# A planned attention-and-gating kernel: own planning keys for early loads, clearing and fillers, and a new table of keys

## The chip, the cores and the metric

The kernel runs on one core of a Trainium2 chip. The metric is the device time of one execution in microseconds, the median of several runs; less is better. The engines are TensorE (PE in the profile; its weight loads are PEld), VectorE (DVE), ScalarE (ACT), GpSimd (POOL) and SyncE (SP), whose queue starts every transfer of this kernel.

## The reference

Sparse attention (8 batches of 8 heads, 576 positions, 64 wide) feeds a gated feed-forward layer that also mixes over positions:

```python
scores = scale * q @ k.T                    # per head
attn   = softmax(where(mask, scores, -1e9)) # 4 heads: the last 32 positions; 4 heads: every 32nd position
x      = (attn @ v) as [8, 576, 512]
h      = relu(x @ w_in)                     # [8, 576, 1024]
u, v   = halves of h
v_n    = (v - mean(v)) / sqrt(var(v) + 1e-6)
v_s    = w_spatial @ v_n + b_spatial        # mixes the 576 positions of a batch
out    = (u * v_s) @ w_out                  # [8, 576, 512]
```

## The kernel before, in words

Two heads are worked together, so a batch has four "head pairs", and head pair t = 4*batch + hp. Pairs 0 and 1 of a batch are local (scores by 36 small products, L507; attn @ v by L617), pairs 2 and 3 are strided (L650 and L720). The softmax of a pair is a chain over DVE and ACT: a reduce for the maximum, exponentials on ACT (L564, L687), a sum, a reciprocal and a product (L469), then a transpose on DVE into the buffer `pc` (L588 local, L704 strided). There is one `pc` buffer, one `ptl` and one `pts`: ACT and POOL copy the transposed blocks into them (L412 on ACT and L414 on POOL are the two forms of one copy), and attn @ v reads them. Its result is moved out of PSUM in two float32r parts, the rounded value (L434, ACT) and what is left (L422, DVE).

Every matrix is kept as such a pair of parts, and a product is three matmuls (`PROD`). Helper `rnd` makes the first part (L412/L414), `rest` the second (L422). The weights arrive as 64-bit words: `words` turns them into float32 by an ACT instruction (L789), a POOL instruction (L798) and a DVE instruction (L806), and `parts` splits them. For w_in there are eight such pieces, for w_out four, from which seven combined blocks are made (`weight_blocks`, L825). `spatial_weights` loads the four row blocks of w_spatial into `wsp_sb`, numbered 0 to 3 here, and the last 64 rows with the bias into `wt_h` and `wt_b` (L905).

A batch has then three stages on PE. Stage 1 (`moe_1`): 4 tiles of v (L957, 128x512), normalised by `chain` (L915, L920 to L940) into `vn`, then 8 tiles of u (L999, 128x288). Stage 0 (`moe_tail`): the last 64 positions. Stage 2 (`moe_2`): `spatial` (L1079, with L1091 and L1092 for the last 64 positions), whose results multiply u on DVE (L1101), then the product with w_out (L1168) in seven partial products, and the stores.

Nothing of the order is written out by hand. Each step is handed to `Program.add` with a key, the engines that could do it with a cost for each, and what it reads and writes. `Program.order` then steps through time with these costs: when an engine is free it takes the ready step with the lowest key, and a step that several engines could do goes where it would end first. `SLOWED` says by how much DVE and POOL steps that run together slow each other. `Program.fillers` looks at the finished plan: where PE would be idle for over `WARM_GAP` before a marked step, it puts products of zeros (L1349, `warm`) ahead of that step, `WARM_SHARE` of the gap long at `WARM_COST` each. What comes out is one fixed order for each engine; on the chip each engine follows its own order and waits where an input is late. The table `KEYS` holds the keys of the first eight head pairs (`a`), of the weight pieces and their loads, of the clearing of buffers (`fill`) and of the steps inside stage 2 (`p`, `b`).

Every load goes through the one SP queue in planned order (`load`, L442), so a load whose buffer is not yet free holds up those behind it.

Of the kernel before, what the change touches and what calls it, by code (L numbers as in the profile page):

```python
# [37 lines left out]
TAIL = S - 4 * P  # L38
NT = 4
KEYS = {  # L40
    "a": (-7906.0, -7964.0, -15830.5, -4267.6, 1379.5, 702.2, 2039.1, -3334.8,),
    "v": (5971.0, -3908.5, -3534.4, 726.2,),
    "u": (4329.4, -8322.8, -3410.6, -6121.6,),
    "s": (13308.3, 1709.1, 5210.5, 13961.2,),
    "t": (2702.5,),
    "o": (1519.5, 3986.0, -8051.8, 12581.5,),
    "cst": (-11921.6,),
    "lead": (-1.3,),
    "fill": (-7688.6, 5328.4, -10489.4, 9430.7, 11172.9, 3859.6,),
    "dp": (12894.8, -1038.4,),  # L50
    "dpt": (657.16,),
    "lv": (-2858.0, -4582.1, -8989.4, -1041.3,),
    "lu": (66.6, -1740.1, -5229.0, 1297.1,),
    "lo": (-7685.9, 12601.4, 4211.2, 6006.6,),
    "ls": (3541.9, 11770.0, 12130.5, 1637.8, 8461.5,),
    "near": (4868.39,),
    "p": (2.79, 10.51, 0.21,),
    "b": (25.62, -1.03, 29.44, -12.2, 10.78, 11.69, 33.63, 25.64, -64.18, 15.47, 14.89,),
}
WARM_END, WARM_GAP, WARM_COST, WARM_COLS, WARM_SHARE = 110000.0, 700.0, 427.0, 256, 0.8  # L60
PE_MASKED, APART = (0, 1, 2, 3), (0, 1)
OTHER_BANK = (1, 2, 3)
FETCHED, FETCH_COST = 100.0, 32.0
SLOWED = ((0.3, 0.15), (0.45, 0.6), (0.9, 0.8))
DMA_RATE, DMA_ISSUE, DMA_LAG, DMA_TAIL, TABLE_LOAD = 370.0, 470.0, 1500.0, 500.0, 1280.0
PROD = ((0, 0), (0, 1), (1, 0))
BLOCKS = ("a11", "a12", "a22", "s1", "s2", "s3", "s4")
# [82 lines left out]
class Program:  # L150
# [39 lines left out]
    def order(self):  # L190
# [14 lines left out]
        held_by = {DVE: (0.0, 0.0, 0, None), POOL: (0.0, 0.0, 0, None)}  # L205
        peer = {DVE: POOL, POOL: DVE}

        def shared(n, e, at, cost):

            if e in self.port.get(n, ()):  # L210
                since, until, share, _ = held_by[peer[e]]
                if since <= at < until:
                    both = min(until - at, cost)
                    slow = SLOWED[max(share, self.share[n])]
                    return (slow[0] * both, slow[1] * both) if e == DVE else (slow[1] * both, slow[0] * both)
            return 0.0, 0.0

# [14 lines left out]
        while len(issued) < len(ops):  # L232
# [57 lines left out]
            if e in self.port.get(n, ()):  # L290
                more, theirs = shared(n, e, now, cost)
                cost += more
                p = peer[e]
                begun, until, share, m = held_by[p]
                if theirs and free[p] == until:
                    free[p] = until = until + theirs
                    held_by[p] = (begun, until, share, m)
                    for j in after[m]:
                        for o in ENGINES:
                            ready_at[j][o] = max(ready_at[j][o], until + LAT[p][o])  # L300
                held_by[e] = (now, now + cost, self.share[n], n)
            free[e] = end = now + cost
            if e == DMA:
                moved = max(moved, now + DMA_LAG) + self.bytes[n] / DMA_RATE
# [13 lines left out]
    def fillers(self, issued):  # L318


        ends, free, found = {}, 0.0, {}
        for at, n, e in issued:
            cost = dict(self.ops[n][1])[e]
            ends[n] = at + cost
            if e == PE:
                if n in self.spare and at < WARM_END:
                    before = self.spare[n][0].before
                    gap = at - max([free, 600.0, *(ends[m] + 200.0 for m in before)])
                    if gap > WARM_GAP:
                        found[n] = int(WARM_SHARE * gap / WARM_COST)  # L330
                free = at + cost
        return found

# [14 lines left out]
def attention_moe(ctx, tc, qT, kT, ks, vl, vs, cst, eye, w_in, w_out, wsp, wtail, out):  # L348
# [91 lines left out]
    def load(key, dst, src, writes, nbytes, reads=()):  # L440
        add(
            key, [(DMA, DMA_ISSUE)], lambda eng: eng.dma_start(dst(), src), reads, writes,  # L442
            size=nbytes,
        )
# [297 lines left out]
    def attention(t, due):  # L742
# [7 lines left out]
            v = lambda: f32(place()).rearrange("p a b c -> p (a b c)").rearrange("p (u d) -> p u d", d=D)  # L750
        else:
            v = place = r_v.new()
        load(due - 34, q, qT[b, hp], [(q,)], P * SP * 4)
        if local:
            k = r_k.new()
            load(due - 33, k, kT[b, hp], [(k,)], P * (STRIDE + S) * 4)
            load(due - 20, lambda: v()[:, : 2 * LB, :], vl[b, hp], [(place,)], P * 768 * 4)
            kin = [(k,)]
        else:
            for j in range(2):  # L760
                load(
                    due - 33, lambda j=j: kbd[j::2, t % 2, j, STRIDE:],
                    ks[b, hp - 2, j], [("k", t % 2, j)], 64 * S * 4, [("k0", t % 2)],
                )
            load(due - 20, v, vs[b, hp - 2], [(place,)], P * 1024 * 4)
            kin = [("k", t % 2, j) for j in range(2)]
        xs[t] = r_x.new()
        (local_attention if local else strided_attention)(t, due, q, k, v, [(place,)], kin)
# [49 lines left out]
    def weight(key, fetch, src, n, dst, tok, stage):  # L818
        val, _, reads = words(key, fetch, src, n, stage)
        parts(key, n, val, dst, reads, tok)  # L820
# [488 lines left out]
    for h in range(2):  # L1309
# [2 lines left out]
            [("k0", h)],  # L1312
        )
        add(
            -90, [(DVE, 250), (POOL, 400)],
            lambda eng, h=h: (
                eng.memset(p_local[h]()[64:, 2 * LS - 2 :, :], 0.0),
                eng.memset(st_local[h]()[64:, NU + 2 * LS - 2 : NU + 2 * LS], 0.0),
# [4 lines left out]
    fill(KEYS["fill"][0], ptl, 2 * LB * LQ, ("ptl0",))  # L1323
    fill(KEYS["fill"][1], pts, NU * 4 * RA, ("pts0",))
    add(-250, [(DVE, 100)], setup_sel, (), [("sel",)])
    add(-100, [(POOL, 1200)], setup_ones, (), [("ones",)])

    def due(t):
        if t < len(KEYS["a"]):
# [104 lines left out]
```

## Time and profile before

| | before |
|---|---|
| time, median of 3 runs | 519.44 us (519.14 to 519.69) |
| the profiled execution | 519.78 us, of which its span is 517.7 us |
| PE busy | 499.6 us of the span |
| DVE, ACT, POOL busy | 363.0, 267.4, 129.0 us |
| moved by transfers | 52.65 MB |

The profile shows one execution. The span runs from the first to the last instruction; the 2.1 us by which the execution's time is longer lie outside it. Rows of the timeline start with the start time and the duration in us, then the engine, the line of the source, what is written and read, the count of merged instructions, and in brackets the idle time of the engine before it and what ended it. A float32r or float32 matmul of the program is one row in the order; a float32 one is two matmuls in the trace.

### The profile page before, as it was taken

The numbers are of one execution on the slowest core, as the hardware profiler recorded it, in microseconds if no ns is written. First come the engines' busy times: TensorE is split into PE (matmuls) and PEld (weight loads), VectorE is DVE, ScalarE is ACT, GpSimd is POOL, SyncE is SP. The second block draws the span as 40 slices with busy tenths as digits, with TensorE's granted clock in tenths as the row PEclk, the third lists the DMA queues.
The fourth block names the chain that finished last, engine by engine and source line by source line (L and its number), as shares of the span: only waits on it lengthen the run. The fifth ranks groups of instructions, "written<-read, shape, count | busy, mean of one in ns | idle before, by whom it ended". The sixth has DMA issues, their size and how long they took to land.

```text
span 517.7 us, 14663 instructions
## 1 busy us (share of the span) xinstructions
PE 499.6 (97%) x5884; PEld 459.3 (89%) x5884; DVE 363.0 (70%) x1093; ACT 267.4 (52%) x825; POOL 129.0 (25%) x245
## 2 busy tenths in 40 slices
PE   6779889999999999999999999999999999999997
PEld 3558779979999899998999899998999889998997
DVE  2899989969479747896369764897457861676156
ACT  5786765568554476456336276366446252233222
POOL 3355864043212121312102111233102120102000
PEclk9689979999999999999999999999999999999999
DMA  8897323454024322262023422063011300020002
GB/s 274 307 343 268 125 83 90 149 164 151 2 79 151 118 79 81 85 180 84 11 69 121 148 80 80 1 209 113 1 56 53 123 1 1 1 80 13 1 1 91
DMA packets 26243, 52.65 MB, mean 102 GB/s; under 512 B 3136, under 2 KB 11584, under 8 KB 26176
## 3 DMA queue, kind: packets, MB, share of 16 engines
q1 hardware_dynamic: 26176, 51.72, 30.3%
q8 instruction: 46, 0.75, 0.6%
q14 instruction: 21, 0.17, 0.1%
HBM read 42.27 MB, written 9.44 MB: 100 GB/s over the span
## 4 chain that ended last, share of the span: by engine, by line
PE 89%; DVE 4%; DMA 2%; ACT 2%; SPq 1%; POOL 1%; issue 1%; POOLq 0%
PE m L1079 20%; PE m L957 18%; PE m L1168 18%; PE m L999 18%; PE po L720 4%; PE po L617 3%; PE s L507 3%; PE s L650 2%; PE m L1091 2%; PE m L1092 2%; DMA k<-kT 1%; SPq L442 1%; DMA x<-wsp 1%; PE po L1349 1%; DVE w_in_sb L422 0%
## 5 line engine op out<-in xcount | busy, mean ns | idle before, releaser
L1079 PE MATMUL m<-wsp_sb,vn 128*128 128x288 f32 x768 | 113.3, 300 | 4.3 <-DVE wsp_sb L422 4.3
L1079 PEld LDWEIGHTS m<-wsp_sb,vn 128*128 128x128 f32 x768 | 107.3, 192 | 5.4 <-DVE wsp_sb L422 4.6
L999 PE MATMUL m<-x,w_in_sb 128*128 128x288 f32 x768 | 105.3, 297 | 0.0
L999 PEld LDWEIGHTS m<-x,w_in_sb 128*128 128x128 f32 x768 | 103.4, 188 | 1.2
L957 PE MATMUL m<-w_in_sb,x 128*128 128x512 f32 (+1 forms) x408 | 99.5, 399 | 0.0
L957 PEld LDWEIGHTS m<-w_in_sb,x 128*128 128x128 f32 (+1 forms) x408 | 74.5, 186 | 19.0 <-DVE x L422 0.2
L1168 PE MATMUL m<-g,w_out_sb 128*128 128x288 f32 x384 | 56.9, 298 | 0.0
L414 POOL TENSOR_SCALAR ptl<-pc 32x64 f32<-32x64 f32 (+3 forms) x89 | 37.9, 426 | 64.7 <-DVE pc L588 24.2
L1168 PEld LDWEIGHTS m<-g,w_out_sb 128*128 128x128 f32 x384 | 52.3, 188 | 1.0 <-ACT vv L434 0.3
L422 DVE TENSOR_TENSOR x<-po,x 128x288 fp32r<-128x288 f32 x64 | 27.6, 447 | 36.3 <-ACT x L434 35.6
L1101 DVE TENSOR_TENSOR u<-m,u 128x288 f32<-128x288 f32 x64 | 28.1, 453 | 30.9 <-PE m L1092 30.7
L564 ACT ACTIVATE pl<-pl,ml 128x64 f32<-128x64 f32 (+1 forms) x140 | 47.0, 339 | 4.7 <-DVE ml L544 4.3
L915 ACT ACTIVATE vv<-m 128x512 f32<-128x512 f32 (+1 forms) x37 | 22.0, 596 | 45.7 <-PE m L957 39.6
L412 ACT CAST g<-u 128x288 fp32r<-128x288 f32 x46 | 19.2, 434 | 50.2 <-DVE u L1101 49.0
L933 POOL TENSOR_TENSOR bn<-bn,sel 128x1 f32<-128x1 f32 (+1 forms) x37 | 21.1, 575 | 95.0 <-DVE bn L928 77.0
L1013 ACT ACTIVATE u<-m 128x288 f32<-128x288 f32 x64 | 25.7, 408 | 35.0 <-PE m L999 34.6
L1168 PE MATMUL m<-vn,w_out_sb 128*128 128x288 f32 x288 | 42.6, 297 | 0.0
L920 DVE BATCH_NORM_STATS2 bn<-vv 128x6 f32<-128x512 f32 (+1 forms) x37 | 25.3, 683 | 21.0 <-ACT vv L915 20.5
L1168 PEld LDWEIGHTS m<-vn,w_out_sb 128*128 128x128 f32 x288 | 39.5, 188 | 0.4
L434 ACT CAST x<-po 128x288 fp32r<-128x288 f32 x64 | 24.7, 397 | 26.2 <-PE po L617 14.4
L412 ACT COPY ptl<-pc 32x64 f32<-32x64 f32 (+3 forms) x103 | 35.7, 346 | 4.7 <-DVE pc L588 2.6
L422 DVE TENSOR_TENSOR g<-u,g 128x288 fp32r<-128x288 f32 x64 | 27.0, 449 | 7.9 <-ACT g L412 6.2
(131 smaller groups left out, 726.6 us busy)
## 6 DMA issues: line engine op xcount, KB each, us to landing
q<-qT SPq DMA_DIRECT2D x30, 295.0 KB, 4.2
outT<-o SPq DMA_DIRECT2D x48, 144.0 KB, 2.7
v_raw<-vs SPq DMA_DIRECT2D x13, 512.0 KB, 4.2
v_raw<-vl SPq DMA_DIRECT2D x16, 384.0 KB, 3.7
k<-kT SPq DMA_DIRECT2D x16, 304.0 KB, 4.5
kbd<-ks SPq DMA_DIRECT2D x32, 144.0 KB, 4.6
outT<-vv SPq DMA_DIRECT2D x16, 144.0 KB, 3.7
vn<-w_in SPq DMA_DIRECT2D x4, 512.0 KB, 4.5
```

Of the source, the lines that this page charges most:

```text
L412: eng.copy(dst(), src())
L414: eng.tensor_scalar(dst(), src(), 1.0, 0.0, op0=ALU.mult, op1=ALU.add)
L422: eng.tensor_tensor(dst(), src(), f32(hi()), op=ALU.subtract)
L434: eng.copy(dst(), src())
L564: eng.activation(p_sb()[:m, u, :], src, AF.Exp, bias=st()[:m, u : u + 1], scale=SCALE if masked else -1.0, **total,)
L920: lambda eng: eng.bn_stats(bn()[:m, 0:6], v()[:m]), [(v,)], [(bn,)],
L957: eng.matmul(v_ps()[:m, :], x_at(kt)[:, a, :], w_in_sb[:, w, kt, HF:], start=(n == 0 and i == 0), stop=(n == NT - 1 and i == 2),)
L999: eng.matmul(u_ps()[:, :HS], w_in_sb[:, w, kt, f * P : (f + 1) * P], xs[NHP * b + kt]()[:, a, r], start=(n == 0 and i == 0), stop=(n == NT ...
L1013: lambda eng, u=u, f=f, u_ps=u_ps: eng.activation(u()[:, f * HS : (f + 1) * HS], u_ps()[:, :HS], AF.Relu),
L1079: eng.matmul(s_ps()[:, :HS], vn()[:, a, kt, fs], wsp_sb[:, w, kt, r], start=(kt == 0 and i == 0), stop=False,)
L1101: lambda eng, ug=ug, s_ps=s_ps: eng.tensor_tensor(ug(), s_ps()[:, :HS], ug(), op=ALU.mult),
L1168: eng.matmul(o_ps()[:, :HS], w_out_sb()[:, b_at, w, kk, a * P : (a + 1) * P], at(j, kk), start=first and kk == 0 and i == 0, stop=kk == 1 ...
```

## The change

`attention` takes the keys of the first loads of the first eight head pairs (q and k from `lq`, v from `lw`) out of the table; before, they were the pair's own key less 34, 33 and 20. The clearing of the local buffers and the setting of the ones in `tails_b` take their keys from `set` (before, -90 and -100), with other POOL costs. `fillers` takes its end, least gap and share from `w`. In the account of the port that DVE and POOL share, a step on POOL that is not a plain copy now counts with weight 2, and the three factors of `SLOWED` are others. All other numbers of `KEYS` are new as well.

```diff
-    "a": (-7906.0, -7964.0, -15830.5, -4267.6, 1379.5, 702.2, 2039.1, -3334.8,),
+    "a": (-9842.3, -13561.9, -6739.1, -5352.0, 1588.0, 1874.9, 6528.0, -115.1,),
...
+    "lq": (-15760.0, -16334.1, -13342.4, -5854.6, 690.8, 3109.9, 6338.5, -4265.1,),
...
+    "set": (3904.8, 1535.2, 5000.2,),
+    "w": (73.2, 1.25, 0.82,),
 }
-WARM_END, WARM_GAP, WARM_COST, WARM_COLS, WARM_SHARE = 110000.0, 700.0, 427.0, 256, 0.8
+WARM_COST, WARM_COLS = 427.0, 256
...
-SLOWED = ((0.3, 0.15), (0.45, 0.6), (0.9, 0.8))
+SLOWED = ((0.45, 0.2), (0.6, 0.5), (0.95, 0.5))
...
+        def weight(n, e):
+            return 2 if e == POOL and self.share[n] else self.share[n]
+
...
-                    slow = SLOWED[max(share, self.share[n])]
+                    slow = SLOWED[max(share, weight(n, e))]
...
-                held_by[e] = (now, now + cost, self.share[n], n)
+                held_by[e] = (now, now + cost, weight(n, e), n)
...
+        until, least, share = KEYS["w"]
...
-                if n in self.spare and at < WARM_END:
+                if n in self.spare and at < until * 1000.0:
...
-                    if gap > WARM_GAP:
-                        found[n] = int(WARM_SHARE * gap / WARM_COST)
+                    if gap > least * 1000.0:
+                        found[n] = int(share * gap / WARM_COST)
...
-        load(due - 34, q, qT[b, hp], [(q,)], P * SP * 4)
+        early = t < len(KEYS["lq"])
+        first = KEYS["lq"][t] if early else due - 34
+        last = KEYS["lw"][t] if early else due - 20
+        load(first, q, qT[b, hp], [(q,)], P * SP * 4)
...
-            -90, [(DVE, 250), (POOL, 400)],
+            KEYS["set"][1 + h], [(DVE, 250), (POOL, 260)],
...
-    add(-100, [(POOL, 1200)], setup_ones, (), [("ones",)])
+    add(KEYS["set"][0], [(POOL, 1060)], setup_ones, (), [("ones",)])
```

The order of the program shows what these numbers do. Line numbers are higher by 8 to 11 after the change, by which L442 becomes L450, L507 L515, L650 L658, L617 L625, L720 L728, L957 L968, L1079 L1090 and L1349 L1360.

The SP queue at the start of the program, before; `w_out_sb` and `xt` lend their room to early q and v, and `vn_101` is where the first piece of w_in lands:

```order
L442 DMA w_out_sb_84<-qT 128x590
L442 DMA xt_87<-vs 128x1024
L442 DMA cst_sb<-cst 128x192
L442 DMA o_97<-eye 128x128
L442 DMA vn_101<-w_in 128x1024
L442 DMA kbd<-ks 64x576 x2
L442 DMA q_123<-qT 128x590
L442 DMA k_134<-kT 128x608
L442 DMA v_raw_140<-vl 128x768
L442 DMA q_176<-qT 128x590
L442 DMA k_181<-kT 128x608
```

The same place after the change; `g_88` is where the first piece of w_in lands:

```order
L450 DMA cst_sb<-cst 128x192
L450 DMA o_85<-eye 128x128
L450 DMA g_88<-w_in 128x1024
L450 DMA q_95<-qT 128x590
L450 DMA k_101<-kT 128x608
L450 DMA q_109<-qT 128x590
L450 DMA k_130<-kT 128x608
L450 DMA xt_138<-vs 128x1024
L450 DMA w_out_sb_178<-qT 128x590
L450 DMA kbd<-ks 64x576 x2
```

The first k of a local pair moves from the ninth transfer to the fifth and the second from the twelfth to the seventh; q, v and the two `kbd` halves of a strided pair, which led, now follow them.

PE early in the program, before, from the end of the second local scores on:

```order
L507 MATMUL s_131<-k_181,q_176 32x64
L1349 MATMUL po_292<-zeros 32x256 x3
L720 MATMUL po_292<-pts,xt_87 64x4x18 x8
L720 MATMUL po_304<-pts,xt_87 64x4x18 x8
L650 MATMUL m_136<-kbd,w_out_sb_84 32x36 x32
L957 MATMUL m_385<-w_in_sb,x_331 128x512 x3
```

The same place after the change:

```order
L515 MATMUL s_127<-k_130,q_109 32x64
L658 MATMUL m_133<-kbd,w_out_sb_178 32x36 x32
L1360 MATMUL po_319<-zeros 32x256 x9
L625 MATMUL po_319<-ptl,v_raw_225 64x96 x6
L625 MATMUL po_339<-ptl,v_raw_225 64x96 x6
L658 MATMUL m_135<-kbd,w_out_sb_178 32x36 x32
L1360 MATMUL po_415<-zeros 32x256 x4
L625 MATMUL po_415<-ptl,v_raw_237 64x96 x6
```

The two local pairs now come first and a strided pair third, where a strided pair was first; thirteen fillers stand between them instead of three (at the very start six instead of eight), and the first tile of v comes after both local pairs.

PE at the start of `spatial` of the first batch, before, from the last product of the tile of the last 64 positions on:

```order
L957 MATMUL m_992<-w_in_sb,x_584 64x512 x3
L1079 MATMUL m_1021<-wsp_sb,vn_768 128x288 x12
L1079 MATMUL m_1042<-wsp_sb,vn_768 128x288 x12
L1079 MATMUL m_1065<-wsp_sb,vn_768 128x288 x12
L1079 MATMUL m_1084<-wsp_sb,vn_768 128x288 x12
```

The same place after the change:

```order
L1090 MATMUL m_1026<-wsp_sb,vn_816 128x288 x3
L1090 MATMUL m_1032<-wsp_sb,vn_816 128x288 x3
L1090 MATMUL m_1038<-wsp_sb,vn_816 128x288 x3
L1090 MATMUL m_1026<-wsp_sb,vn_816 128x288 x9
L1090 MATMUL m_1032<-wsp_sb,vn_816 128x288 x9
L1090 MATMUL m_1038<-wsp_sb,vn_816 128x288 x9
L1090 MATMUL m_1091<-wsp_sb,vn_816 128x288 x12
```

The three products of row block 0 of w_spatial are taken first for three of the tiles, nine in all, and row blocks 1 to 3 follow; before, each tile took its twelve products in one go.

More of the change, by code (lines that the diff above doesn't have):

```diff
@@ L40 @@
 KEYS = {
-    "a": (-7906.0, -7964.0, -15830.5, -4267.6, 1379.5, 702.2, 2039.1, -3334.8,),
[L42 to L58, printed above, removed]
+    "a": (-9842.3, -13561.9, -6739.1, -5352.0, 1588.0, 1874.9, 6528.0, -115.1,),
+    "v": (3324.6, -3241.3, 9582.3, -5209.5,),
+    "u": (1292.4, -8773.3, 1053.3, -7394.3,),
+    "s": (2510.3, 5363.0, 3093.9, 7327.8,),
+    "t": (3012.2,),
+    "o": (3704.2, 5299.5, -4144.6, 3282.7,),
+    "cst": (-27014.0,),
+    "lead": (-1.28,),
+    "fill": (831.9, 1735.9, -6584.2, 7746.1, -10956.1, -3358.7,),
+    "dp": (10150.7, -1069.6,),
+    "dpt": (1659.05,),
+    "lv": (-3549.0, -10121.4, -23802.2, 253.8,),
+    "lu": (-1364.4, 547.0, -7064.7, 2152.9,),
+    "lo": (1371.6, 1303.1, 10963.2, -2623.4,),
+    "ls": (11951.3, 14222.0, 7837.0, 4330.3, 14728.9,),
+    "near": (7082.92,),
[4 rows of a table added]
+    "set": (3904.8, 1535.2, 5000.2,),
+    "w": (73.2, 1.25, 0.82,),
 }
-WARM_END, WARM_GAP, WARM_COST, WARM_COLS, WARM_SHARE = 110000.0, 700.0, 427.0, 256, 0.8
+WARM_COST, WARM_COLS = 427.0, 256
 PE_MASKED, APART = (0, 1, 2, 3), (0, 1)
@@ L752, in attention @@
             v = place = r_v.new()
-        load(due - 34, q, qT[b, hp], [(q,)], P * SP * 4)
+        early = t < len(KEYS["lq"])
+        first = KEYS["lq"][t] if early else due - 34
+        last = KEYS["lw"][t] if early else due - 20
+        load(first, q, qT[b, hp], [(q,)], P * SP * 4)
         if local:
             k = r_k.new()
-            load(due - 33, k, kT[b, hp], [(k,)], P * (STRIDE + S) * 4)
-            load(due - 20, lambda: v()[:, : 2 * LB, :], vl[b, hp], [(place,)], P * 768 * 4)
+            load(first + 1, k, kT[b, hp], [(k,)], P * (STRIDE + S) * 4)
+            load(last, lambda: v()[:, : 2 * LB, :], vl[b, hp], [(place,)], P * 768 * 4)
             kin = [(k,)]
@@ L761, in attention @@
                 load(
-                    due - 33, lambda j=j: kbd[j::2, t % 2, j, STRIDE:],
+                    first + 1, lambda j=j: kbd[j::2, t % 2, j, STRIDE:],
                     ks[b, hp - 2, j], [("k", t % 2, j)], 64 * S * 4, [("k0", t % 2)],
                 )
-            load(due - 20, v, vs[b, hp - 2], [(place,)], P * 1024 * 4)
+            load(last, v, vs[b, hp - 2], [(place,)], P * 1024 * 4)
             kin = [("k", t % 2, j) for j in range(2)]
```

3 rows, old and new, of the table KEYS are left out of this document.

## Prediction

> **What bounds the kernel now.** I read the busy shares first, then PE's share and clock over the span.
>
> ```profile
> PE 499.6 (97%) x5884; PEld 459.3 (89%) x5884; DVE 363.0 (70%) x1093; ACT 267.4 (52%) x825; POOL 129.0 (25%) x245
> PE   6779889999999999999999999999999999999997
> PEclk9689979999999999999999999999999999999999
> ```
>
> PE is busy nearly everywhere; what it lacks lies in the first six of the 40 slices, where the clock is reduced too. The busy times of four stretches (PE, PEld, DVE, ACT, POOL, then clock and transfers) say who is short there.
>
> ```profile
> 0.00:25.00 25.00, 18.03 (x352) 11.54 (x354) 12.29 (x32) 15.71 (x42) 9.22 (x24) 0.80 0.82 288
> 25.00:67.00 42.00, 34.63 (x467) 29.07 (x462) 41.27 (x111) 32.44 (x92) 27.88 (x38) 0.94 0.71 246
> 67.00:86.00 19.00, 18.79 (x197) 18.46 (x198) 17.50 (x40) 10.43 (x36) 10.27 (x15) 0.87 0.27 83
> 86.00:518.00 432.00, 428.16 (x4876) 400.19 (x4874) 291.91 (x914) 208.85 (x658) 81.64 (x169) 1.00 0.24 78
> ```
>
> From 86 us on PE misses 3.84 us, which is the end of the program (last results out and stored). From 25 to 67 us DVE is busy 41.27 of 42 us: it sets the pace of the ramp, and PE waits. PE's own waits show where they meet.
>
> ```profile
> PE m L1079 <- DVE wsp_sb L422: 4.3, 1, 4.3
> ```
>
> PE's timeline around that one wait, and DVE's:
>
> ```profile
> 59.87 2.94 PE L957 MATMUL m<-w_in_sb,x 128*64 128x512 f32 x12
> 62.64 0.29 PE L1079 MATMUL m<-wsp_sb,vn 128*128 128x288 f32 x1
> 67.21 8.65 PE L1079 MATMUL m<-wsp_sb,vn 128*128 128x288 f32 x47 [4.28 <-DVE wsp_sb L422]
> ```
> ```profile
> 65.75 2.08 DVE L422 TENSOR_TENSOR wsp_sb<-x,wsp_sb 128x576 fp32r<-128x576 f32 x3
> ```
>
> I call 67.21 the gate: PE has done stage 1 of the first batch and sits until DVE has made the low part of row block 0 of w_spatial, the second of the three rests that start at 65.75. From the gate on PE never waits for long. So the time is the gate, plus the PE work behind it.
>
> **Behind the gate nothing changes but eight matmuls.** The PE order after the change holds the same work on both sides of the gate; only that nine products of row block 0 now stand ahead of the wait (one was there before), and 39 instead of 47 follow. In later batches, at full clock, 48 matmuls of 512 columns and 96 of 288 columns (the size of these nine) take this long, in the chain of work that ended last:
>
> ```profile
> 231.84 11.20 PE m L957 x48
> 243.04 12.79 PE m L999 x96
> ```
>
> 12.79/96 = 0.133 us (and 11.20/48 = 0.233 for the wide ones), so the gate's far side is 8 x 0.133 = 1.07 us shorter. The later stages take slightly different orders with the new `p` and `b`, around which PE had no idle time (428.16 of 432 us with the end counted); DVE has 292 of 432 us of work there, so I count them at nothing. If that cover were gone, each wait for a late part would cost its own length, and seven changeovers from stage 2 to stage 1 would show it.
>
> **The gate is DVE's work plus its idle and lengthened time.** Up to the gate DVE has 142 instructions in both orders, of the same kinds, except that one rest of w_spatial has gone to POOL and the rest for `wt_b` has come ahead of the gate, both 0.74 us long. Before, the gate is the 141st of them, after it is the 142nd: 0.67 us (start to start) is lost there. So the question is how much sooner the start gets DVE going, and whether it is disturbed more.
>
> Before, DVE's start is this:
>
> ```profile
> 7.85 0.69 DVE L806 SCALAR_TENSOR_TENSOR vn<-vn 128x512 int32<-128x512 int32 x1 [6.96 <-POOL vn L798]
> 12.56 0.49 DVE L527 TENSOR_REDUCE ml<-m 128x5 f32<-128x320 f32 x1 [1.54 <-PE m L507]
> 27.52 0.78 DVE L422 TENSOR_TENSOR x<-po,x 128x288 fp32r<-128x288 f32 x2
> ```
>
> Adding the unhindered start-to-start times of each kind (0.60 us for 128x512, 0.37 for 288 columns, 0.76 for a local transpose and so on), the work ahead of the row at 27.52 is worth 13.3 us, and that up to the second rest 43.8. What is done by 27.52 before equals what the new order has done with its 33rd DVE row, the transpose of the first strided pair. When is that reached? These rows carry it, first the k's transfer (KB each, us to landing):
>
> ```profile
> k<-kT SPq DMA_DIRECT2D x16, 304.0 KB, 4.5
> ```
> ```profile
> 2.57 0.43 SPq L442 DMA_DIRECT2D vn<-w_in  x1
> 6.17 0.43 SPq L442 DMA_DIRECT2D k<-kT  x1
> 7.59 0.43 SPq L442 DMA_DIRECT2D k<-kT  x1
> 11.20 1.34 PE L507 MATMUL m<-k,q 64*32 64x64 f32 x72 [1.65 <-DMA k<-kT]
> 13.82 1.12 PE L507 MATMUL s<-k,q 64*32 64x64 f32 x59 [1.27 <-DMA k<-kT]
> 14.06 2.10 ACT L564 ACTIVATE pl<-m,ml 128x64 f32<-128x64 f32 x10 [2.50 <-DVE ml L535]
> 25.29 0.81 DVE L469 TENSOR_TENSOR pl<-pl,ml 128x640 f32<-128x640 f32 x1
> 27.62 2.54 ACT L412 COPY ptl<-pc 32x320 f32<-32x320 f32 x7
> 24.67 1.28 PE L617 MATMUL po<-ptl,v_raw 128*64 128x96 f32 x24 [0.32 <-POOL g L798]
> ```
>
> The first k was issued at 6.17 and its scores began at 11.20, 5.03 us on; the second k took 6.2 us (7.59 to 13.82). The fifth transfer of a queue that doesn't wait is issued where the w_in piece stood, at 2.57, the seventh 0.94 later, at 3.51. So the local scores begin at about 7.6 and 9.7 instead of 11.2 and 13.8. The maxima follow 1.36 us behind (9.0 and 11.1, with 0.9 us of DVE each), the exponentials at 10.2 to 12.3 and 12.3 to 14.4 (2.10 per set), sum, reciprocal and product (0.73, 0.13, 0.81 start to start) by 14.3, the second sum by 15.3, the first transpose by 16.0. Its thirteen block copies, split between ACT and POOL, take 2.5 us, so the second transpose can start at 18.7, since there is one `pc`. The first attn @ v starts at 18.9 and ends at 20.2; the second copies follow, behind ACT's two casts of the first result, until 23.7, and the 33rd DVE row runs from 23.8 to 24.45. That is 3.07 us ahead of 27.52. The clearing of `pts` goes from ACT to POOL, ahead of the first word step there:
>
> ```profile
> 2.11 2.17 POOL L1290 MEMSET kbd<- 128x1216 f32 x2
> 7.14 0.64 POOL L798 TENSOR_SCALAR vn<-vn 128x512 int32<-128x512 uint8 x1 [2.85 <-DMA vn<-w_in]
> ```
>
> POOL was done clearing at 4.28 and waited 2.85 us for the piece; about 1.1 us more ends at 5.4, ahead of the piece, which now lands near 6.2, so it costs nothing. Of the queue's late half, the loads that wait for PE (the k of the third local pair, the v of the fourth) land six or more us ahead of their use.
>
> From there the rest of the way is 43.8 - 13.3 = 30.5 us of DVE work before; it took from 27.52 to the gate's rest, which ends 0.3 us ahead of 67.21, so 39.4 us, 1.29 for each. What lengthens it is POOL:
>
> ```profile
> 42.02 1.75 POOL L422 TENSOR_TENSOR wsp_sb<-x,wsp_sb 128x576 fp32r<-128x576 f32 x1
> 42.39 1.92 DVE L422 TENSOR_TENSOR w_in_sb<-vn,w_in_sb 128x512 fp32r<-128x512 f32 x1
> 15.62 0.92 POOL L414 TENSOR_SCALAR pts<-pc 32x288 f32<-32x288 f32 x2 [7.84 <-DVE pc L704]
> 54.06 1.00 POOL L414 TENSOR_SCALAR wt_h<-x 128x576 fp32r<-128x576 f32 x1
> ```
>
> The DVE rest of 0.60 us took 1.92, to just after POOL's rest had ended. Up to the gate POOL has one rest of w_spatial more after the change (1.75), a copy for w_in more and one for vn less, no `wt_h` (-1.00), and two `pts` copies less (0.46 each): together about nothing. I keep 1.29. The Trainium skill (SBUF — State Buffer, "SBUF: two separate sides") says that of a DVE step with two SBUF inputs and a POOL step that reads SBUF, whichever starts first holds a port pair for its whole length and the other is fully blocked. The row at 42.39 agrees: 0.60 us of work ended 0.55 us behind POOL's. By this rule the added POOL rest speaks against the change and costs up to 1.75 us more: a gate at 66.8 and a time of 518.0.
>
> So the gate comes at 24.45 + (30.5 + 0.67) x 1.29 + 0.3 = 65.0 us, 2.2 sooner. PE itself gets there at about 61.8: the last v tile needs the w_in and x rests at DVE's 51st and 54th rows (10.6 us of work on, 24.45 + 10.6 x 1.29 = 38.1), then 15 v matmuls at 0.233, 96 of u at 0.133, a strided attn @ v and local scores 2.05, its wait for `pts` 1.3, the tail tile 2.8 and nine products 1.2. It then idles 3.2 us instead of 4.28, so I leave the slow clock behind the gate as it is.
>
> **The sum.** 519.78 (profiled execution) - 2.2 (gate) - 1.07 (eight matmuls) = 516.5. The median of before lies 0.34 below its profiled run, so **516.2 us**. The loads may land 0.5 us sooner (4.5 us is the k's median) or 1 us later, and the factor may lie between 1.18 and 1.35, the latter with the whole POOL rest added (41.15/30.5). Sooner and 1.18 give a gate at 61.0, but PE is not there before 61.6; later and 1.35 give 67.8. That makes 512.8 to 519.0 for this case.
>
> **Rivals.** (A, chance 0.57) The sum above, faster. (B, 0.13) The lengthening shrinks, since the new plan charges more for the overlaps, to 1.18 or less: the gate then falls to 24.45 + 31.2 x 1.18 + 0.3 = 61.6, where PE arrives, its wait and the slow matmuls behind it go (47 in 8.65 us instead of 6.26, so 2.4 us): about 511 to 513 (519.78 - 5.6 - 1.07 - 0.34 = 512.8, and 510.4 with all of the slow clock gone). For it speaks the many DVE rows of 0.9 us and more for 0.5 us of work; against it, that POOL has as much to do. (C, 0.13) The lead of 3 us is lost again by the gate, because the later loads, behind PE's releases, come no sooner: only -1.07 + 0.67, so 519.4 and, on the median, 519.0, no change. Against it: from 25 us on DVE was idle for 0.73 of 42 us only, so it was not waiting for loads there.
>
> (D, 0.17) Slower: the fillers run at half clock and overrun the gap they fill. Nine calls, 18 matmuls, stand ahead of the first attn @ v, and four more ahead of the second.
>
> ```profile
> 3.50 0.18 PEld L1349 LDWEIGHTS m<-zeros 128*32 128x32 f32 x1 [0.25 <-issue]
> 3.88 1.62 PEld L1349 LDWEIGHTS m<-zeros 128*32 128x32 f32 x8 [0.21 <-issue]
> ```
> ```profile
> 16.39 0.46 PE L507 MATMUL s<-k,q 64*32 64x64 f32 x13 [1.45 <-issue]
> 16.78 2.77 PE L1349 MATMUL po<-zeros 128*32 128x256 f32 x6
> 19.48 1.88 PE L720 MATMUL po<-pts,xt 128*64 128x72 f32 x32
> ```
>
> Before, six of them took 2.77 us, 0.46 each, and the product behind them began at 19.48, though POOL's copies for it ended at 16.54: about two us were lost there already. With the strided scores done at 12.5 and a stall like the 1.45 us at 16.39, 18 at 0.46 last from 14.0 to 22.3, 3.4 us past the 18.9 above, and eight more cost another us: DVE's 33rd row then ends at 28.85, the gate comes at 69.4, and the time is 519.78 + 2.2 - 1.07 - 0.34 = 520.6. Against it: at the very start the first fillers came 0.43 apart and, from 3.88 on, eight in 1.62 us (0.20 each), so a long run of fillers speeds up; at seven slow and eleven fast ones it takes 5.2 us, and the overrun is 0.3 us with the stall and none without it. The case decides from about 0.3 us per filler on. The Trainium skill (TensorE: Matmul & The Clock Gate, "Part 1: The HAM clock gate") states that the clock stays at half until PE has been busy for a window of about 3.4 us. The change of pace at 3.88, some 3 us after the first filler, agrees, and by this rule nine calls take 3.4 us at half pace and 2.0 at full, 5.4 in all, and D does not happen.
>
> **Chances.** A measurement here can tell about 0.2% (1.0 us) from no change. Faster by more: A and B, 0.70. Within: C, 0.13. Slower by more: D, 0.17. The range leaves out the lower half of B and the upper half of D (0.15 together, and what A's ends leave out): 511.6 to 520.6.
>
> **What would show it.** The local scores start near 7.6 and 9.7; DVE's transpose of the first strided pair ends near 24.5; the rest of row block 1 of w_spatial ends near 64.7 and PE goes on near 65.0 with 39 matmuls; from 86 us on PE misses nothing but its 3.8 us end. A late first attn @ v behind a long filler row shows D; a gate at 67 with an early start shows C; a gate near 61.6 with no PE wait shows B. I would be wrong altogether if PE waited anywhere behind the gate, at the changeovers or for the w_out blocks, whose transfers now start when DVE's two rests ahead of the gate free their buffers.

## The result, and the profile after

The changed kernel takes **522.64 us** (median of 7 runs, 521.43 to 523.46); the kernel before, beside it on the same chip, 519.67 us. The ratio is 1.0059, with a 95% interval from 1.0038 to 1.0080: slower by 0.6%, or 3 us. The profiled execution took 523.46 us, with a span of 521.4.

The page of the changed kernel, busy shares and the two rows of PE's share and clock:

```profile
PE 503.0 (96%) x5900; PEld 458.5 (88%) x5900; DVE 365.4 (70%) x1088; ACT 263.4 (51%) x816; POOL 135.8 (26%) x259
PE   6888979999999999999999999999999999999997
PEclk9798999999999999999999999999999999999999
```

The four stretches of the prediction, for the changed kernel (PE, PEld, DVE, ACT, POOL, then clock and transfers):

```profile
0.00:25.00 25.00, 18.84 (x348) 10.67 (x350) 13.34 (x34) 16.25 (x48) 11.19 (x27) 0.86 0.76 279
25.00:67.00 42.00, 37.50 (x490) 31.46 (x486) 34.17 (x104) 30.34 (x83) 26.05 (x36) 0.96 0.67 240
67.00:86.00 19.00, 16.33 (x191) 15.54 (x192) 17.93 (x43) 11.62 (x39) 7.29 (x13) 1.00 0.35 109
86.00:518.00 432.00, 430.25 (x4877) 400.81 (x4875) 299.48 (x909) 205.17 (x648) 91.32 (x184) 1.00 0.24 77
```

Two rows have changed character. From 25 to 67 us DVE is no longer full (34.17 of 42 us, 41.27 before). And in the last stretch DVE and POOL are busier than before, by 7.6 and 9.7 us (291.91 and 81.64 then), for the same batches.

Where was the time lost? PE's first product with w_out of batch 0 is a good cut: ahead of it lies the ramp, behind it seven and a half batches at full pace. It begins here before and after the change:

```profile
86.27 1.76 PE L1168 MATMUL m<-g,w_out_sb 128*128 128x288 f32 x12
```
```profile
86.45 1.75 PE L1179 MATMUL m<-g,w_out_sb 128*128 128x288 f32 x12
```

So in these two profiles the ramp gained nothing (0.18 us later), and what follows takes 521.4 - 86.45 = 434.95 us instead of 517.7 - 86.27 = 431.43: 3.5 us lost where I had counted nothing.

**The ramp.** PE's timeline of the changed kernel (start, length, line, count, and in brackets the idle time before it and its cause):

```profile
7.32 0.97 PE L515 MATMUL m<-k,q 64*32 64x64 f32 x72
9.16 0.96 PE L515 MATMUL s<-k,q 64*32 64x64 f32 x72 [0.87 <-DMA k<-kT]
15.20 0.35 PE L658 MATMUL m<-kbd,w_out_sb 128*32 128x36 f32 x9 [2.56 <-issue]
15.34 5.97 PE L1360 MATMUL po<-zeros 128*32 128x256 f32 x18
21.24 1.21 PE L625 MATMUL po<-ptl,v_raw 128*64 128x96 f32 x24
24.79 1.21 PE L625 MATMUL po<-ptl,v_raw 128*64 128x96 f32 x24
32.31 4.46 PE L968 MATMUL m<-w_in_sb,x 128*128 128x512 f32 x18 [1.30 <-issue]
42.43 5.54 PE L968 MATMUL m<-w_in_sb,x 128*128 128x512 f32 x16 [2.14 <-issue]
62.85 2.92 PE L968 MATMUL m<-w_in_sb,x 128*64 128x512 f32 x12
65.61 0.96 PE L1090 MATMUL m<-wsp_sb,vn 128*128 128x288 f32 x6
67.35 0.79 PE L1090 MATMUL m<-wsp_sb,vn 128*128 128x288 f32 x4 [0.78 <-ACT u L1024]
69.13 5.33 PE L1090 MATMUL m<-wsp_sb,vn 128*128 128x288 f32 x38 [0.98 <-DVE wsp_sb L430]
75.79 0.40 PE L1102 MATMUL m<-wt_h,tail 128*128 128x288 f32 x1 [1.34 <-DVE tail L430]
```

The local scores start even sooner than predicted. Then the 18 fillers run from 15.34 to 21.24, and only then comes the first attn @ v. DVE meanwhile runs dry, and its 33rd row, the transpose, ends at 26.17 instead of 24.45:

```profile
22.43 0.46 DVE L430 TENSOR_TENSOR x<-po,x 128x288 fp32r<-128x288 f32 x1 [2.53 <-ACT x L442]
25.47 0.70 DVE L712 STREAM_TRANSPOSE pc<-pp 128x512 f32<-128x512 f32 x1
```

PE loses 1.30 and 2.14 us more to two stalls that nothing in the profile ends (32.31 and 42.43, "issue"). It comes to the first products of `spatial` at 65.61 (61.8 predicted) and passes the gate at 69.13, 1.9 us later than before. Behind the gate it makes the time up: 38 matmuls in 5.33 us (0.140 each; before, 47 in 8.65, 0.184 each). Its wait there was 0.98 us instead of 4.28, and the granted clock from 67 to 86 us was 1.00 instead of 0.87.

### The profile page after: what moved, and what is told of

Its sections match the earlier page's. It is cut to its first block, busy times and chain, and to the rows that moved or that the text cites. A ratio compares the mean times of both kernels' runs of the same rounds, so it can differ in the third digit from the quotient of the medians.

```text
span 521.4 us, 14687 instructions
## 1 busy us (share of the span) xinstructions
PE 503.0 (96%) x5900; PEld 458.5 (88%) x5900; DVE 365.4 (70%) x1088; ACT 263.4 (51%) x816; POOL 135.8 (26%) x259
## 4 chain that ended last, share of the span: by engine, by line
PE 83%; DVE 9%; DMA 3%; ACT 2%; issue 2%; POOL 1%; SPq 0%; ACTq 0%; DVEq 0%; POOLq 0%
PE m L968 20%; PE m L1010 18%; PE m L1090 17%; PE m L1179 13%; PE po L728 4%; PE po L625 2%; PE s L515 2%; DVE vn L430 2%; DMA kbd<-ks 2%; PE m L1102 2%; PE s L658 2%; PE m L1103 1%; DMA x<-wsp 1%; PE po L1360 1%; DVE o L836 1%
## 5 line engine op out<-in xcount | busy, mean ns | idle before, releaser
L1090 PE MATMUL m<-wsp_sb,vn 128*128 128x288 f32 x768 | 111.3, 296 | 1.8 <-DVE wsp_sb L430 1.0
L1090 PEld LDWEIGHTS m<-wsp_sb,vn 128*128 128x128 f32 x768 | 105.3, 189 | 3.0 <-DVE wsp_sb L430 1.2
L968 PE MATMUL m<-w_in_sb,x 128*128 128x512 f32 (+1 forms) x408 | 101.3, 401 | 3.4 <-issue 3.4
L968 PEld LDWEIGHTS m<-w_in_sb,x 128*128 128x128 f32 (+1 forms) x408 | 75.0, 187 | 22.6 <-issue 4.3
L422 POOL TENSOR_SCALAR ptl<-pc 32x320 f32<-32x320 f32 (+3 forms) x91 | 35.8, 393 | 62.3 <-DVE pc L596 38.0
L420 ACT CAST g<-u 128x288 fp32r<-128x288 f32 x49 | 20.6, 433 | 50.0 <-DVE u L1112 47.6
L931 DVE BATCH_NORM_STATS2 bn<-vv 128x6 f32<-128x512 f32 (+1 forms) x37 | 25.4, 689 | 17.0 <-ACT vv L926 16.4
L422 POOL TENSOR_SCALAR vn<-u 128x288 fp32r<-128x288 f32 x20 | 9.3, 477 | 94.2 <-DVE u L836 78.0
L442 ACT CAST x<-po 128x288 fp32r<-128x288 f32 x64 | 24.9, 399 | 16.9 <-PE po L625 8.3
```

Of the source, the lines that this page charges most:

```text
L420: eng.copy(dst(), src())
L422: eng.tensor_scalar(dst(), src(), 1.0, 0.0, op0=ALU.mult, op1=ALU.add)
L442: eng.copy(dst(), src())
L931: lambda eng: eng.bn_stats(bn()[:m, 0:6], v()[:m]), [(v,)], [(bn,)],
L968: eng.matmul(v_ps()[:m, :], x_at(kt)[:, a, :], w_in_sb[:, w, kt, HF:], start=(n == 0 and i == 0), stop=(n == NT - 1 and i == 2),)
L1090: eng.matmul(s_ps()[:, :HS], vn()[:, a, kt, fs], wsp_sb[:, w, kt, r], start=(kt == 0 and i == 0), stop=False,)
```

## The experiments

Seventeen kernels were run. Each is compared with the kernel before, run beside it on the same chip, whose medians lay between 518.85 and 519.21 us. Beside the changed kernel it took 519.67, so gains over the changed kernel are read from the ratios (its own is 1.0059) and not from the bare times. "Behind" is the span less the start of the first w_out product, as above.

**Keys of stage 2, taken back and put in alone.** e1, the changed kernel with two lines of `KEYS` as before:

```
-    "p": (3.03, 9.82, 1.12,),
-    "b": (75.04, 18.29, 19.61, 0.69, 3.12, 18.44, 36.18, 14.65, -122.99, 8.37, 12.39,),
+    "p": (2.79, 10.51, 0.21,),
+    "b": (25.62, -1.03, 29.44, -12.2, 10.78, 11.69, 33.63, 25.64, -64.18, 15.47, 14.89,),
```

> The changed kernel with the old keys `p` and `b` (spacing and due times of the steps of stage 2); everything else as changed. Theory K (these keys cost the time behind the ramp): the first w_out products begin near 86.5 us as before, and from there to the end it takes about 431.5 us as in the kernel before instead of 434.95, so 519 us, 3 us less than the changed kernel. Rival F (the ramp's fillers decide, the later stages only follow): from 86.5 us on still about 435 us, time 522 to 523. Rival P (the mended port account moves steps to POOL and lengthens DVE's in every batch, whatever the keys): still 434 us or more, 522.

Measured: 519.56 us, ratio 1.0004 [0.9980, 1.0029]; behind 432.5 us. e2 is the reverse, the kernel before with those two lines as changed.

> The kernel before with the new keys `p` and `b` alone. Theory K: the ramp as before (products of w_out from about 86.3 us), the rest 3 us longer (434.5 instead of 431.4 us), time 522 to 523, 0.6% slower than before. Rival P (the port account): about the time of before, 519 to 520, since the account is the old one. Rival F: 519 to 520 too.

Measured: 522.47 us, ratio 1.0082 [1.0059, 1.0104]; behind 434.7 us. So these two lines cost about 3 us, in the changed kernel and in the one before. Behind the ramp it is 2.4 us in the one (434.95 against 432.5) and 3.3 us in the other (434.7 against 431.4).

**The late fillers.** e3 is the changed kernel with only the fillers of the very start:

```
-    "w": (73.2, 1.25, 0.82,),
+    "w": (14.0, 1.25, 0.82,),
```

> The changed kernel with only the 12 filler matmuls at the very start; the 18 ahead of the first attn @ v and the 8 ahead of the second are left out (they write nothing that is read). If the fillers delay the start (the slower rival D of the prediction): the first attn @ v begins near 18.5 us instead of 21.2, DVE's 33rd row ends some 2 us sooner than 26.1, and if the lead lasts PE goes on with row block 1 of w_spatial near 67 instead of 69.1, time 520.5. If the lead is lost later (w_in words, ACT's order, the code stalls): first attn @ v early, but the w_out products of the first batch again at 86 to 87 us and the time 522 to 523. If a slower clock follows from missing fillers: attn @ v and v products up to about 30 us at half pace, and 523 or more.

Measured: 518.11 us, ratio 0.9989 [0.9971, 1.0006], which is 0.7% or 3.6 us under the changed kernel's 1.0059. PE's timeline of e3:

```profile
15.86 0.35 PE L658 MATMUL m<-kbd,w_out_sb 128*32 128x36 f32 x9 [2.76 <-issue]
17.46 2.19 PE L625 MATMUL po<-ptl,v_raw 128*64 128x96 f32 x24 [1.25 <-POOL ptl L422]
64.42 6.85 PE L1090 MATMUL m<-wsp_sb,vn 128*128 128x288 f32 x38 [2.73 <-DVE wsp_sb L430]
81.63 1.75 PE L1179 MATMUL m<-g,w_out_sb 128*128 128x288 f32 x12
```

The first attn @ v runs at 17.46 instead of 21.24, at a slower pace (2.19 us instead of 1.21), and the gate is passed at 64.42. DVE's two rows that the prediction named, in e3:

```profile
23.35 0.71 DVE L712 STREAM_TRANSPOSE pc<-pp 128x512 f32<-128x512 f32 x1
63.61 0.75 DVE L430 TENSOR_TENSOR wsp_sb<-x,wsp_sb 128x576 fp32r<-128x576 f32 x1
```

From the end of the one to the end of the other are 40.3 us for 31.2 us of work: a factor of 1.29, the figure assumed. It is made up differently, as the busy times on this way show (the kernel before, from the point that the prediction matched with that transpose, then e3), with DVE's three longest waits in e3:

```profile
27.59:67.16 39.57, 32.04 (x377) 27.06 (x377) 38.89 (x108) 30.06 (x87) 28.04 (x38) 0.93 0.69 239
```
```profile
24.06:64.36 40.30, 36.73 (x470) 31.50 (x470) 36.75 (x108) 32.94 (x100) 26.72 (x35) 0.96 0.71 254
```
```profile
DVE w_out_sb L430 <- POOL w_out_sb L422: 1.3, 1, 1.3
DVE vn L817 <- POOL vn L809: 0.8, 1, 0.8
DVE w_in_sb L430 <- POOL w_in_sb L422: 0.7, 1, 0.7
```

Before, DVE was busy all the way (38.89 of 39.57 us). In e3 it is busy for 36.75 us, so its work is lengthened by 1.18 only, and it is idle for 3.55, mostly in waits for POOL. The last of them (1.34 us, up to 63.27) stands just ahead of the gate's rest.

e8 halves the late fillers:

```
-                        found[n] = int(share * gap / WARM_COST)
+                        found[n] = int((share if at < 5000.0 else 0.5 * share) * gap / WARM_COST)
```

> The changed kernel with half of the late fillers: 8 matmuls instead of 18 ahead of the first attn @ v, 4 instead of 8 ahead of the second; the 12 of the start stay. If it is the overrun past the moment at which the first attn @ v could start (about 18.2 us) that costs: 8 at 0.43 us from 15.3 end at 18.8, so it starts near 18.8 and the time is within 1 us of the kernel without late fillers, 518 to 519. If fillers in this place cost by their mere presence (their own code, the clock, or a swap of order): half the cost, about 520.3. If these 26 matmuls had nothing to do with it: 522.6.

Measured: 518.29 us, ratio 0.9975 [0.9961, 0.9988], as good as none, with the first w_out product at 82.97. PE's timeline of e8:

```profile
15.88 3.61 PE L1360 MATMUL po<-zeros 128*32 128x256 f32 x8
19.42 1.83 PE L625 MATMUL po<-ptl,v_raw 128*64 128x96 f32 x20
```

Eight fillers end about when the copies are done, so it is the overrun past that point that costs, not the fillers as such. How much of a delay is free isn't sharp: the product is 2 us later than in e3 and the time is the same.

The two stalls of the changed kernel's ramp (32.31 and 42.43) are absent in e3, but they are not the fillers' price. Six other kernels below have all the fillers and the changed kernel's order up to the gate, and neither stall (e6, e9, e11, e13, e16, e17). They wait 2.7 us for DVE at the gate, as e3 does, and pass it at 66.38 to 69.60 us, against 64.42 in e3 and 64.74 in e5. In them DVE's 33rd row ends at 26.15 to 27.77 us, in these two at 24.06 and 23.87.

e7 takes the six late fillers out of the kernel before (`WARM_END` 14000 instead of 110000).

> The kernel before with its six late filler matmuls (16.78 us, ahead of its first strided product) left out; the 16 of the start stay. If an overrunning filler row delays the ramp whatever the order: these six took 2.77 us, about two of them behind the copies that the product waits for, so w_out products begin up to 2 us sooner than 86.3 and the time is 517 to 518. If DVE's work sets that ramp (it was busy 41.27 of 42 us), the gate stays at 67 and the time at 519.

Measured: 518.44 us, ratio 0.9980 [0.9962, 0.9998], 0.2% faster, between the two forecasts. Its gate is passed at 66.62 us, behind a wait for DVE of 3.50 us. With the old start order DVE's work sets the ramp, and little is to be had there.

**The port account.** e4 puts the old `SLOWED` and weights back in the changed kernel:

```
-SLOWED = ((0.45, 0.2), (0.6, 0.5), (0.95, 0.5))
+SLOWED = ((0.3, 0.15), (0.45, 0.6), (0.9, 0.8))
-            return 2 if e == POOL and self.share[n] else self.share[n]
+            return self.share[n]
```

> The changed kernel with the port account of before (old SLOWED, POOL's rounding copies weighed as DVE's); keys as changed. Theory K: still some 434 to 435 us behind the first w_out products, 521 to 523 (the order of the ramp shifts from DVE's 35th row on, by up to 2 us either way). Rival P: POOL gets fewer steps, DVE's rows in stage 2 are not lengthened, 431.5 us behind 86.5, time about 519.

Measured: 525.1 us, ratio 1.0119 [1.0093, 1.0145]; first w_out product at 89.45, behind 434.65. Rival P is out: the account changes nothing behind the ramp. With these keys the new account makes the better ramp.

**Both costs taken out.** e5 has e1's and e3's edits.

> The changed kernel with both edits of the first two experiments: the old keys `p` and `b`, and only the 12 filler matmuls of the very start. If the two costs lie in different stages they add up: w_out products of the first batch from about 81.6 us (as without the fillers alone), then 432 us as with the old keys alone, a profiled span of 513.6 and a time of about 515.3, 0.7% faster than before. If the fillers' 4.5 us were gained only because the new keys leave something to gain, or the old keys only help a late ramp: 518 or more.

Measured: **516.4 us**, ratio 0.9943 [0.9923, 0.9963], faster than both kernels; behind 432.4 us. By the ratios the gains of e1 and e3 over the changed kernel are 0.55% and 0.70%, together 1.25%; e5 gains 1.16%, or 6.0 us. Within the intervals the two costs add up, as costs of two different stages should. The forecast of 515.3 us was 1.1 us too low.

**Which of the keys.** Four runs, each the changed kernel with the part named put back: e6 the spacing (third number of `p`), e9 all of `p`, e10 all of `b`; in e11 the steps of stage 2 (288 columns) may not go to POOL:

```
+        two = n == HS
...
+            key, n, lambda: dst(0), val, reads, [(*tok, 0)], (ACT, DVE) if two else (ACT, DVE, POOL),
...
+            (DVE,) if two else (DVE, POOL), port=(DVE, POOL),
...
-            key, [(DVE, 70 + 1.04 * n), (POOL, 200 + 2.0 * n)],
+            key, [(DVE, 70 + 1.04 * n)] + [(POOL, 200 + 2.0 * n)] * (n != HS),
```

> The changed kernel with one number put back: the spacing of the fourteen product steps of stage 2, the third number of `p`, 0.21 instead of 1.12; the other two of `p` and all of `b` as changed. If the spacing is what costs (products of w_out in long runs behind parts that DVE makes just then): as with all of `p` and `b` put back, 432 us behind 86 us, time about 519.5. If the due times in `b` cost: still 434 to 435 us, time 522 to 523.

> The changed kernel with all three numbers of `p` put back (how far the second half's products of row blocks, and the products with w_out, stand behind the first), and `b` as changed. Putting back the spacing alone left 436 us behind the first w_out product. If the three of `p` together decide what runs beside what: about 432 us behind 86, time 519.5. If the due times in `b` are what costs: 434 to 436 us, 522 to 523.5. If it is the count of stage 2's rounding copies and differences on POOL that costs, this order, which has few there, comes out at 519.5 as well.

> The changed kernel with the old due times `b`, and `p` as changed: the other half. If `p` decides: still 434.5 to 435 us behind 86.5, 522.5. If `b` decides: 432 us and 519.5. If POOL's share of stage 2 costs (this order keeps its five differences and its many copies there): 522.5.

> The changed kernel with new keys and fillers, but stage 2's rounding copies, rests and differences (288 columns wide) may not be placed on POOL; ACT and DVE make them all. Theory P2 (POOL's steps there hold up DVE's rows of two SBUF inputs, so parts of w_out products and freed PSUM come late): DVE's rows for o<-u,u fall back from 0.65 to 0.48 us, the waits on DVE's sums go, 432 us behind 86.5, time 519 to 520. Rival O (it is the order of the steps, and POOL's share is only a companion): 434 to 435 us, 522 to 523. If ACT and DVE lack the room: 436 or more, 524.

Measured: e6 523.76 us (behind 436.5), e9 519.48 (432.9), e10 522.39 (435.7), e11 522.37 (434.3). So `p` decides and `b` does not; my guess that it is the spacing alone fell, and so did the theory that POOL's share of stage 2 is the cause (in e11 it has no such step).

e12 to e14 looked for the wait and for one single number; e12 lets the sums of stage 2 go first on DVE:

```
-                key, [(DVE, 70 + 1.04 * HS)],
+                key - 40.0, [(DVE, 70 + 1.04 * HS)],
```

> The changed kernel with one edit: the sums of stage 2 on DVE (w_out products plus an earlier result, which free PSUM for the next product into the same bank) get keys 40 lower, so that they go ahead of whatever else DVE has ready; all keys in the table as changed. Theory W (with the new `p` these sums stand behind other DVE steps, and the next product waits for them: twice 0.47 us flagged, the rest as gaps too short to be flagged): the waits on these sums are gone and of 434.7 us behind the first w_out product 1.5 to 2.5 us go: 520 to 521. If the sums are only a sign: still 434 to 435 us and 522 to 523.

> The changed kernel with the first number of `p` put back, 2.79 instead of 3.03 (how far the second half's products of row blocks stand behind the first's). If this number decides: 432 us behind the first w_out product, 519.5. If not: 434 to 436 us, 522 to 523. This order has none of stage 2's differences on POOL.

> The changed kernel with the second number of `p` put back, 10.51 instead of 9.82 (how far the w_out products stand behind stage 2's start). If this number decides (products called 0.7 us too early for their parts): 432 us behind the first w_out product, 519.5. If not: 434 to 436 us, 522 to 523. If neither this nor the first one does it alone, only the three together make an order without the waits.

Measured: 522.48, 522.28 and 522.7 us (behind 435.6, 434.4, 434.8). None of the three is enough. In e12 the sum still came late, after the same neighbours, as DVE's and PE's rows show:

```profile
281.75 0.44 DVE L674 SCALAR_TENSOR_TENSOR pp<-s,cst_sb 128x288 f32<-128x288 f32 x1
282.23 0.45 DVE L683 TENSOR_REDUCE mx<-pp 128x16 f32<-128x288 f32 x1
282.60 0.45 DVE L1207 TENSOR_TENSOR o<-m,vv 128x288 f32<-128x288 f32 x1
283.10 2.13 PE L1179 MATMUL m<-vn,w_out_sb 128*128 128x288 f32 x14 [0.47 <-DVE o L1207]
```

A lower key moves a step only ahead of others that the plan has ready with it. Here DVE is back to back, and I take it to be simply behind the plan.

e15 to e17 put back two of the three numbers each.

> The changed kernel with the second and third number of `p` put back (10.51 and 0.21), the first as changed (3.03). Theory S (two costs, either of which is enough: w_out products called 0.7 us too early when close together, or spread over 14.6 us so that the last ones stand among the next stage's products; the first number is idle): about 432 us behind the first w_out product, 519.5. Rival T (all three make the one order without waits): 434 to 436 us, 522 to 523.

> The changed kernel with the first and third number of `p` put back (2.79 and 0.21), the second as changed (9.82). Theory S: the products are called too early, 434 to 436.5 us, 522 to 524. Rival T: the same. If the second number is idle and first and third decide: 432 us, 519.5.

> The changed kernel with the first and second number of `p` put back (2.79 and 10.51), the spacing as changed (1.12). Theory S: the spread products cost, 434 to 435 us, 522 to 523. Rival T: the same. If the spacing is idle and first and second decide: 432 us, 519.5.

Measured: e15 522.97 us over five executions, ratio 1.0072 [1.0050, 1.0095] (a sixth, the profiled one, took 2701.77 us, so its trace says nothing here), e16 519.45, ratio 1.0002 [0.9987, 1.0017], behind 431.9; e17 522.97 (436.1). So the first and the third number decide, each alone enough to cost the time, and the second is idle where the other two are old (e16). That the new first number costs its time behind the ramp is shown by e6, which differs from e15 in the second number alone. Theory S had the right form with the wrong member: two separate costs, one of them the spacing, the other the first number (3.03, how far the second half's row blocks stand behind the first's) and not the second.

All kernels but e15 fall into two groups, by `p` alone:

| first and third of `p` | kernels | behind the first w_out product | waits of PE on DVE's sums listed there |
|---|---|---|---|
| both old (2.79, 0.21) | before, e1, e5, e7, e9, e16 | 431.4 to 432.9 us | none |
| one or both new | after, e2, e3, e4, e6, e8, e10 to e14, e17 | 434.0 to 436.5 us | 2 to 4, together 0.6 to 1.9 us |

The list of PE's waits has this row in the changed kernel, and none like it in the first group:

```profile
PE m L1179 <- DVE o L1207: 0.9, 2, 0.5
```

That list has only the longer waits. So I add up from the traces, behind the first w_out product, by how much each matmul that another engine's semaphore released began later than the usual spacing of its kind (0.133 us for 288 columns), where that is over 0.04 us. It makes 0.7 to 0.9 us in the first group and 2.5 to 4.7 us in the second. In the second, DVE's sums are the largest part of it, 1.6 to 2.8 us; in the first they make 0.1 to 0.5. Between the kernels before and after it is 2.0 of the 3.5 us (0.7 and 2.7). The rest of the 3.5 us are gaps that nothing in the profile ends, in which the two groups overlap (14.5 to 15.8 us and 15.4 to 16.4 us in all).

What stands behind one such wait is shown by the stage 2 in which it falls. The first 7.5 us of it, before, in the changed kernel, and in e16:

```profile
272.80:280.30 7.50, 7.46 (x129) 6.89 (x128) 7.34 (x19) 6.46 (x19) 2.79 (x8) 1.00 0.28 86
```
```profile
274.60:282.10 7.50, 7.50 (x131) 7.15 (x130) 7.32 (x15) 5.74 (x16) 5.82 (x12) 1.00 0.36 133
```
```profile
272.80:280.30 7.50, 7.50 (x132) 7.20 (x130) 6.86 (x19) 5.13 (x15) 1.89 (x4) 1.00 0.12 42
```

DVE has little or no time to spare in all three (7.34, 7.32 and 6.86 of 7.5 us), but in the changed kernel it gets 15 instructions done where the others get 19, while POOL is busy 5.82 us instead of 2.79 or 1.89. These rows show part of it (POOL, then DVE and PE, of the changed kernel):

```profile
275.39 1.00 POOL L836 TENSOR_TENSOR u<-u 128x288 f32<-128x288 f32 x1
```
```profile
275.65 1.06 DVE L836 TENSOR_TENSOR o<-u,u 128x288 f32<-128x288 f32 x1
276.63 1.66 DVE L430 TENSOR_TENSOR vn<-u,vn 128x288 fp32r<-128x288 f32 x3
282.28 0.45 DVE L1207 TENSOR_TENSOR o<-m,vv 128x288 f32<-128x288 f32 x1
282.79 2.66 PE L1179 MATMUL m<-vn,w_out_sb 128*128 128x288 f32 x18 [0.47 <-DVE o L1207]
```

POOL does one of the differences; DVE's next one takes 1.06 us instead of 0.45 and ends 0.32 us after POOL's; its next three take 1.66 us. Some five us later DVE's sum comes too late for the product that waits for it. The Trainium skill (SBUF — State Buffer, "SBUF: two separate sides") lets the one that starts second wait for the whole of the first, and this row agrees. But taking POOL away (e11) gives DVE that work back, and the time is no better; e13, whose order has none of stage 2's differences on POOL, is no better either. I read this as stage 2 having no slack on DVE, so that an order that lets it fall behind costs, by whichever engine. That is argued from this one stage and these two kernels; no run gave DVE slack there.

**What stays open.** Where the time goes is shown, by the sums above. Why just these two numbers tip the plan was not followed through the planner.

## Why the prediction was wrong

Forecast 516.2 us, measured 522.64, outside the range and on the other side. Two steps failed: the first attn @ v was computed too early, and the later stages were counted at nothing. By its own steps:

- **The start: right.** Local scores at 7.32 and 9.16 (7.6 and 9.7 predicted).
- **The first attn @ v at 18.9: wrong, by the fillers.** This is rival D, to which I gave 0.17. I had the fillers begin at 14.0 and take 5.2 us. They began at 15.34, as the stall ahead of them was 2.56 us and not 1.45, and took 5.97. And the copies were done sooner: e3 runs the product at 17.46, though its stall ended 0.66 us later (15.86 instead of 15.20). PE's weight loads show the pace:

```profile
15.75 0.18 PEld L1360 LDWEIGHTS po<-zeros 128*32 128x32 f32 x1 [0.25 <-issue]
18.74 0.18 PEld L1360 LDWEIGHTS po<-zeros 128*32 128x32 f32 x1 [0.25 <-issue]
19.17 1.66 PEld L1360 LDWEIGHTS po<-zeros 128*32 128x32 f32 x8 [0.25 <-issue]
```

  They come 0.43 us apart until 19.17 and 0.21 apart from there, so D's reason (half pace throughout) was not the reason: the mean was 0.33 us, just past the 0.3 from which I had let D decide. The Trainium skill (TensorE: Matmul & The Clock Gate, "Part 1: The HAM clock gate") gave 5.4 us for the row by its window of 3.4 us; here the slow part lasted 4.1 us (15.34 to 19.42), and the granted clock came back at 19.23. The page leaves room for that by saying that the window runs freely.
  D's gate, 69.4 us, is close to the 69.13 of the profile, but by luck: D had the 33rd row end at 28.85 (measured 26.17), and the two stalls of 1.30 and 2.14 us, which it did not know of, made up for that.
- **DVE as the pace of the ramp, factor 1.29: the number held, by luck.** e3 shows 1.29 and a gate at 64.42 (65.0 predicted), and the six kernels with all fillers and without the two stalls show 1.28 to 1.35. But DVE was not full, as the step had it: in e3 its work was lengthened by 1.18, the figure of rival B, and the rest were waits, mostly for POOL, which the prediction had put at nothing. In the changed kernel's own profile, with the stalls, the factor was 1.38 and DVE was busy 34.17 of 42 us.
- **Eight matmuls earlier, 1.07 us: right in kind, small in size.** From the gate to the first w_out product it is 17.3 us after (86.45 - 69.13) and 19.1 before (86.27 - 67.21). In e3 it is 17.2 us, with matmuls behind the gate as slow as before (38 in 6.85 us, 0.180 each). So nine matmuls fewer, 38 instead of 47, at this slow pace make 1.8 us; the prediction had taken eight at full clock. In the changed kernel's own profile the 38 took 5.33 us, but PE then waited 1.34 us for the tail.
- **"I count them at nothing": wrong, 3.5 us between the two profiles and 2.9 us by the ratios (e1).** I argued from PE's 428.16 of 432 us that the later stages have cover. That says how full PE was with the old order, not how far each DVE step was from being late. The same row showed DVE at 292 of 432, an average over stages; in the first 7.5 us of stage 2 DVE was busy 7.34. The prediction did name a PE wait behind the gate as what would make it wrong altogether.

With both costs taken out, e5 measures 516.4 us. That this is close to the forecast is in part luck too, as the factor was right for the wrong reason.

## What to carry to other kernels

A bottleneck engine that never waits is only as safe as the busiest helper in the tightest stage: before a new order is counted at nothing, look at the helper's share window by window, not over the span. Filler work is free only while it ends before the real work is ready; here half of it cost nothing, and none at all did as well. And where a table of numbers is replaced as a whole, put its parts back one group at a time: the good and the bad of this one lay in different groups.

## What the runs showed of the hardware that was not expected

The ramp of one and the same order varies by some 4 us from execution to execution. As far as lines, tiles and shapes in the traces tell, nine kernels give every engine the same order as the changed kernel until past the first w_out product (e1, e6, e9, e10, e12 to e14, e16, e17). With the changed kernel that makes ten profiles of one ramp, and the product comes at 84.23 us at the earliest (e10) and at 88.16 at the latest (e14):

```profile
84.23 1.75 PE L1179 MATMUL m<-g,w_out_sb 128*128 128x288 f32 x12
```

One profile's start is therefore known to about 4 us; the 86.45 of the changed kernel is the eighth of the ten. The three profiles with half or none of the late fillers lie ahead of all ten (81.63, 82.97, 83.04). The part behind lay within 1.5 us in the first group above and 2.5 us in the second, whose orders differ more. The verdicts rest on medians of 5 to 12 executions.

In every trace of the changed start, PE stalls for 2.3 to 3.3 us ahead of the 56th small product of the first strided scores (2.56 in the changed kernel, 2.76 in e3), with no wait in the profile to explain it. This product is PE's 222nd matmul in the trace. In the kernels with the old start PE stalls ahead of its 222nd matmul too, for 0.7 to 1.5 us, though that is another product there. The two stalls of the changed kernel at 32.31 and 42.43 us, where they appear in other kernels with its start, stand ahead of the 474th and the 601st.

The traces also hold transfers of 16384 bytes on a queue that the profile calls "instruction". In the changed kernel one ends at 13.75, one at 30.87 and one at 40.92 us, each 1.4 to 1.5 us before PE goes on (15.20, 32.31, 42.43). Of 40 stalls of PE over 0.25 us that nothing else explains, in all traces but e15's, 39 end 1.25 to 1.59 us behind the end of such a transfer. This fits PE waiting for its own instructions, but it is a coincidence in time; no run took it apart.
